# Opening of a fused attention and feed-forward kernel: one load queue in order of need, tile 1 normalised on ScalarE, tiles 2 and 3 transposed on TensorE

## The chip, the cores and the metric

The kernel runs on one core of one Trainium2 chip. The core has five engines that run their own instruction lists in order and meet through semaphores: TensorE (PE in the profile, with its weight loads listed apart as PEld), VectorE (DVE), ScalarE (ACT), GpSimd (POOL) and SyncE (SP, which here only issues transfers). The metric is the device time of one execution, in microseconds; lower is better.

## The reference

An input x of 2048 rows by 512 columns (bf16) is layer-normalised to xn. The result is x, plus a linear attention of xn, plus a gated feed-forward block of xn:

```python
xn = layernorm(x)
q, k, v = split(xn @ wqkv)                      # 32 heads of 16
phi = lambda t: where(t > 0, t + 1, exp(t)) + 1e-6
kv  = phi(k)^T v ;  z = sum over rows of phi(k) # per head
o   = (phi(q) kv) / (phi(q) z + 1e-6)
out = x + o @ wo + (silu(xn @ w_gate) * (xn @ w_up)) @ w_down   # hidden size 1792
```

The attention isn't causal: kv and z are sums over all 2048 rows, so they are known only after the last row.

## The kernel before, in words

The rows are cut into 16 tiles of 128 rows (t = 0 to 15). The work has two stages.

In the first, every tile is normalised and transposed, its K and Q projections are computed, and sums over the rows are gathered. In the second, the feed-forward block runs over 4 chunks of 512 rows (ffn, lines 545 to 575), and output tiles follow behind each chunk (outtile, line 754). The change touches only the opening of the first stage.

A small recorder, `_Prog`, takes operations in program order. K.op(engine, functions, r, w) appends them to the list of one engine and works out from the names read and written which semaphores the engine has to wait for; K.dma does the same for a transfer on the queue of an engine. No planner reorders anything: each engine runs its list in the order in which the program calls came, and a waiting instruction holds up all that stands behind it on its engine.

The steps of one tile, with their lines:

- xload (193) and wqkv_load (199) issue the transfers of x and of the K and Q weights (wk, wq, each in two halves of 256 KB). Before, they alternate between the queues of SP and ACT; the load of tiles 4 and 5 waits for tiles 0 and 1.
- stat(t) (467) is three steps: bns (274) and agg (277) on DVE give mean and variance; rstd_pow (290) gives 1/sqrt(variance + 1e-5) in two POOL instructions, vpe (an addition, line 294; for tile 0 on DVE) and rstd (a power, line 301).
- xn_dve (280) normalises the tile on DVE: (x - mean) * rstd. Tile 0 does so in two halves (xn_half, 323).
- The transposed tile xnT comes from PE and a copy out of PSUM on ACT (transpose_pe, 305, four 128x128 blocks; for tile 0 transpose_half, 333), or from a DMA transpose on SP's queue (transpose_dma, 351). Before, tiles 0 to 2 go through PE, the others by DMA; xn(t) (472) is xn_dve and, from tile 3 on, the DMA.
- kproj and qproj (391, 394) are four PE products of 512 columns each, one for each 128 rows of the weight. kb(t) and qb(t) name their PSUM banks, which alternate between 0, 1 and 2, 3.
- exp_k (397) and exp_q (403) on ACT read the banks, feat_k (431) on DVE finishes the K feature and frees the K bank, zsum (442) on POOL adds it up, gtacc (454) on PE accumulates xn^T phi(k) in banks 4 to 7.
- fill issues products on a tile of zeros (idle), whose results nobody reads.

The order of the opening is written out by hand (lines 477 to 505): statistics of tiles 0 and 1, both halves of tile 0, tile 1's normalising, statistics of 2 and 3, tile 2's normalising; then PE's list; then a loop over tiles with two tables, STAT and XN, that say behind which tile the later statistics and normalisings are issued.

Of the kernel before, what the change touches and what calls it, by code (L numbers as in the profile page):

```python
# [6 lines left out]
ACT = mybir.ActivationFunctionType  # L7
ALU = mybir.AluOpType
AX = mybir.AxisListType

P = 128
# [3 lines left out]
NT = S // P  # L15
# [93 lines left out]
def bass_parallel_sum__linear_attn_block__swiglu_ffn__prompt_kernel(  # L109
# [12 lines left out]
    K = _Prog()  # L122
    pe, act, dve, pool, sp = nc.tensor, nc.scalar, nc.vector, nc.gpsimd, nc.sync
    bf, f32 = dt.bfloat16, dt.float32

    with contextlib.ExitStack() as es:
        E = es.enter_context

        def sb(name, shape, d=bf):
            return E(nc.sbuf_tensor(name, [P] + shape, d))  # L130

        x_sb = sb("x_sb", [NT, D])
        xn_sb = sb("xn_sb", [NT, D])
# [10 lines left out]
        mv = sb("mv", [NT, 2], f32)  # L144
        vpe = sb("vpe", [NT], f32)
        rstd = sb("rstd", [NT], f32)
        nb = sb("nb", [NT], f32)
# [1 line left out]
        ek = sb("ek", [NE, D])  # L149
        eq = sb("eq", [NT, D])  # L150
        warm = sb("warm", [1], f32)
        idle = sb("idle", [512])
        pkq = sb("pkq", [NT, 2, D])
        zacc = sb("zacc", [D], f32)
        zhi = sb("zhi", [D])
# [19 lines left out]
        banks = [psum[:, i, :] for i in range(8)]  # L175
# [10 lines left out]
        def bk(i):  # L186
            return ("bank", i)
# [5 lines left out]
        def xload(eng, h, t0, n, after=()):  # L193
            K.dma(
                eng, lambda: h.dma_start(x_sb[:, t0:t0 + n, :], xv[:, t0:t0 + n, :]),
                r=list(after), w=[("x", t0 + i) for i in range(n)],
            )

        def wqkv_load(eng, h, name, i, c0, n):
            K.dma(  # L200
                eng,
                lambda: h.dma_start(
                    wqkv_sb[:, c0:c0 + n, i * D:(i + 1) * D],
                    A_wqkv[c0 * P:(c0 + n) * P, i * D:(i + 1) * D].rearrange("(c p) f -> p c f", p=P),
                ),
                w=[(name, c0)],
            )
# [4 lines left out]
        def wpiece(name, dst, src, c):  # L212
            K.dma("sp", lambda: sp.dma_start(dst[:, c, :], src[c * P:(c + 1) * P, :]), w=[(name, c)])

        xload("sp", sp, 0, 1)
        xload("act", act, 1, 1)
        wqkv_load("sp", sp, "wk", 1, 0, 2)
        wqkv_load("act", act, "wk", 1, 2, 2)
        xload("sp", sp, 2, 1)
        xload("act", act, 3, 1)  # L220
        wqkv_load("sp", sp, "wq", 0, 0, 2)
        wqkv_load("act", act, "wq", 0, 2, 2)
        xload("sp", sp, 4, 2, [("x", 0), ("x", 1)])
        xload("sp", sp, 6, 4)
        xload("sp", sp, 10, 2)
        xload("sp", sp, 12, 4)
# [8 lines left out]
                out=ident[:, :], in_=ident[:, :], compare_op=ALU.not_equal, fill=1.0,  # L235
                base=0, pattern=[[-1, P]], channel_multiplier=1,
            ),
            r=[("ident",)], w=[("ident",)],
        )
        K.op("pool", lambda: pool.memset(nhalf[:, :], -0.5), w=[("nhalf",)])  # L240
        K.op("dve", lambda: dve.memset(idle[:, :], 0.0), w=[("idle",)])

        def fill(n, after):
            K.op(
                "pe",
                [
                    (lambda: pe.matmul(banks[3], idle[:, 0:P], idle[:, :], start=True, stop=True))
                    for _ in range(n)
                ],
                r=[("idle",)] + after, w=[bk(3)],  # L250
            )

        def masks():
# [20 lines left out]
        def bns(t):  # L274
            K.op("dve", lambda: dve.bn_stats(stats[:, t, :], x_sb[:, t, :]), r=[("x", t)], w=[("st", t)])  # L275
# [4 lines left out]
        def xn_dve(t):  # L280
            K.op(
                "dve",
                lambda: dve.tensor_scalar(  # L283
                    out=xn_sb[:, t, :], in0=x_sb[:, t, :], scalar1=mv[:, t, 0:1], scalar2=rstd[:, t:t + 1],
                    op0=ALU.subtract, op1=ALU.mult,
                ),
                r=[("x", t), ("mv", t), ("rstd", t)], w=[("xn", t)],
            )

        def rstd_pow(t):  # L290
# [14 lines left out]
        def transpose_pe(t, b):  # L305
            tb = banks[b].bitcast(bf)[:, 0:512].rearrange("p (c s) -> p c s", c=NDC)
            K.op(
                "pe",
                [
                    (lambda c=c: pe.transpose(tb[:, c, :], xn_sb[:, t, c * P:(c + 1) * P], ident[:, :]))  # L310
                    for c in range(NDC)
                ],
                r=[("xn", t), ("ident",)], w=[bk(b)],
            )
            K.op(
                "act",
                lambda: act.activation(xnT[:, :, t * P:(t + 1) * P], tb, ACT.Copy),
                r=[bk(b)], w=[("xnT", t)],
            )
# [52 lines left out]
        def proj_half(t, b, lo, wname, h):  # L372
            K.op(
                "pe",
                [
                    (lambda c=c: pe.matmul(
                        banks[b], xnT[:, c, t * P:(t + 1) * P], wqkv_sb[:, c, lo:lo + D],
                        start=(c == 0), stop=(c == NDC - 1),
                    ))
                    for c in (2 * h, 2 * h + 1)  # L380
                ],
                r=[("xnTh", t, h), (wname, 2 * h)], w=[bk(b)],
            )

        def kb(t):
            return 2 * (t % 2)

        def qb(t):
            return 2 * (t % 2) + 1

        def kproj(t):
            proj(t, kb(t), D, "wk")

        def qproj(t):
            proj(t, qb(t), 0, "wq")

        def exp_k(t):
            K.op(
                "act", lambda: act.activation(ek[:, t % NE, :], banks[kb(t)], ACT.Exp),  # L399
                r=[bk(kb(t))], w=[("ek", t % NE)],  # L400
            )

        def exp_q(t):
            K.op(
                "act", lambda: act.activation(eq[:, t, :], banks[qb(t)], ACT.Exp),
                r=[bk(qb(t))], w=[("eq", t)],
            )
            K.op(
                "act", lambda: act.activation(pkq[:, t, 1, :], banks[qb(t)], ACT.Copy),
                r=[bk(qb(t))], w=[("pq", t)],  # L410
            )
# [19 lines left out]
        def feat_k(t):  # L431
            e = t % NE
            clip(ek[:, e, :], ("ek", e))
            if t >= 1:
                zsum(t - 1, e)
            maxadd(pkq[:, t, 0, :], banks[kb(t)], ek[:, e, :], [bk(kb(t)), ("ek", e)], [("pk", t)])
# [17 lines left out]
        def gtacc(t):  # L454
            K.op(
                "pe",
                [
                    (lambda c=c: pe.matmul(  # L458
                        banks[4 + c], xn_sb[:, t, c * P:(c + 1) * P], pkq[:, t, 0, :],
                        start=(t == 0), stop=(t == NT - 1),  # L460
                    ))
                    for c in range(NDC)
                ],
                r=[("xn", t), ("pk", t)], w=[bk(4 + c) for c in range(NDC)],
            )

        def stat(t):
            bns(t)
            agg(t)
            rstd_pow(t)  # L470

        def xn(t):
            xn_dve(t)
            if t >= 3:
                transpose_dma(t)

        stat(0)
        stat(1)
        xn_half(0, 0)
        xn_half(0, 1)  # L480
        xn_dve(1)
        stat(2)
        stat(3)
        xn_dve(2)

        fill(10, [])
        fill(1, [("mv", 0)])
        fill(1, [("rstd", 0)])
        transpose_half(0, 4, 0)
        transpose_half(0, 5, 1)  # L490
        fill(1, [])
        proj_half(0, kb(0), D, "wk", 0)
        proj_half(0, kb(0), D, "wk", 1)
        exp_k(0)
        transpose_pe(1, 6)
        qproj(0)
        exp_q(0)
        transpose_pe(2, 7)
        kproj(1)
        qproj(1)  # L500
        feat_k(0)
        xn(3)

        STAT = {0: (4, 5), 1: (6,), 2: (7,), 3: (8,), 4: (9, 10), 5: (11,), 6: (12,), 7: (13,), 8: (14, 15)}
        XN = {0: (4,), 1: (5,), 2: (6,), 3: (7,), 4: (8,), 5: (9, 10), 6: (11,), 7: (12,), 8: (13,), 9: (14, 15)}

        for t in range(NT):
            if t >= 2:
                kproj(t)
            if t >= 1:  # L510
                exp_k(t)
            if t >= 2:
                qproj(t)
            if t >= 1:
                exp_q(t)
                feat_k(t)
            for i in STAT.get(t, ()):
                stat(i)
            for i in XN.get(t, ()):
                xn(i)  # L520
            if t in (2, 4, 6, 8):
                wpiece("wg", wg_sb, B_w_gate, t // 2 - 1)
            if t == 11:
                for c in range(NDC):
                    wpiece("wu", wu_sb, B_w_up, c)
                wqkv_load("sp", sp, "wv", 2, 0, 4)
                wload("sp", sp, "wo", wo_sb, A_wo)
            if t == 14:
                wload("sp", sp, "wd", wd_sb, B_w_down)
            if t == 12:  # L530
                masks()
            if t >= 2:
                gtacc(t - 2)
        zsum(NT - 1, None)
        gtacc(NT - 2)
# [292 lines left out]
```

## Time and profile before

| | |
|---|---|
| median of 3 runs | 214.36 us (214.14 to 215.16) |
| profiled execution | 214.34 us, span of instructions 213.0 us |
| PE busy | 207.5 us (97%), 972 instructions |
| DVE, ACT, POOL busy | 119.4, 67.6, 72.6 us |
| moved by DMA | 16.32 MB, mean 77 GB/s |
| tile 0 of x landed | 3.3 us after its issue at 0.80 |
| first product of a projection | 7.10 us |
| granted TensorE clock | 1.00 in all 40 slices |

Times in the profile count from the first instruction. In a timeline a line gives start, length, engine, line of the kernel, operation, what is written and read, and in brackets how long the engine stood idle before and who released it. A product on PE is pipelined: its own length is 0.38 us, but the next one starts 0.216 us later, so the pitch of a group tells PE's rate. DVE and ACT overlap the start-up of neighbouring instructions in the same way.

### The profile page before, as it was taken

How to read it: one execution, taken by the hardware profiler on the slowest of the kernel's cores; microseconds unless marked ns; L12 is line 12 of the kernel's file. 1: busy time of each engine (PE TensorE's matmuls, PEld its weight loads, DVE VectorE, ACT ScalarE, POOL GpSimd, SP SyncE). 2: the span in 40 equal slices, each digit the busy share in tenths (PEclk: the TensorE clock that was granted, in tenths of full speed). 3: DMA queues.
4: the chain of work that ended last, by engine and by line, in shares of the span. 5: the costliest groups of instructions: out<-in, count | busy, mean ns of one | idle time of the engine just before them, and what ended most of it. 6: DMA issues, size and time to landing. Idle time of an engine off the chain costs nothing.

```text
span 213.0 us, 2744 instructions
## 1 busy us (share of the span) xinstructions
PE 207.5 (97%) x972; PEld 96.0 (45%) x991; DVE 119.4 (56%) x241; ACT 67.6 (32%) x117; POOL 72.6 (34%) x95
## 2 busy tenths in 40 slices
PE   7899999999999999999999999999999999999995
PEld 2344444444544444444444444444444444444454
DVE  2899997333544776446373746464556536364121
ACT  2576666667353332213122302112032213121000
POOL 1559996646013444032130442131414131221100
PEclk9999999999999999999999999999999999999999
DMA  5924598899102011110101011101011010110201
GB/s 188 388 65 125 139 143 207 287 368 266 26 0 52 0 25 25 49 24 28 31 20 49 3 35 39 49 0 49 3 49 25 25 25 28 49 25 26 51 28 51
DMA packets 26671, 16.32 MB, mean 77 GB/s; under 512 B 18592, under 2 KB 25120, under 8 KB 26656
## 3 DMA queue, kind: packets, MB, share of 16 engines
q1 hardware_dynamic: 25824, 15.34, 27.1%
q10 hardware_dynamic: 832, 0.79, 1.2%
q8 instruction: 8, 0.13, 0.3%
q14 instruction: 7, 0.06, 0.1%
HBM read 9.70 MB, written 2.10 MB: 55 GB/s over the span
## 4 chain that ended last, share of the span: by engine, by line
PE 94%; DVE 2%; DMA 2%; issue 1%; POOL 1%; DVEq 0%
PE psum L550 45%; PE psum L733 23%; PE psum L363 12%; PE psum L722 6%; PE psum L458 6%; DMA x_sb<-in_A_x_dram 2%; DVE stats L275 1%; POOL rstd L301 1%; PE psum L648 0%; PE psum L671 0%; DVE xn_sb L283 0%; DVE mv L278 0%; POOL vpe L294 0%; DVE out_sb L746 0%; PE psum L310 0%
## 5 line engine op out<-in xcount | busy, mean ns | idle before, releaser
L565 ACT ACTIVATE sg<-psum 128x512 bf16<-128x512 f32 x56 | 33.4, 598 | 106.8 <-PE psum L550 106.0
L550 PE MATMUL psum<-xnT,wu_sb 128*128 128x512 bf16 x222 | 57.4, 379 | 0.1
L550 PE MATMUL psum<-xnT,wg_sb 128*128 128x512 bf16 x217 | 56.0, 379 | 0.4
L680 POOL TENSOR_TENSOR prod<-pkq,zb 128x512 f32<-128x512 bf16 x16 | 18.6, 1161 | 57.8 <-DVE pkq L425 57.8
L550 PEld LDWEIGHTS psum<-xnT,wu_sb 128*128 128x128 bf16 x224 | 21.9, 98 | 26.4
L550 PEld LDWEIGHTS psum<-xnT,wg_sb 128*128 128x128 bf16 x224 | 21.9, 98 | 26.2
L746 DVE TENSOR_TENSOR out_sb<-psum,x_sb 128x512 bf16<-128x512 f32 (+1 forms) x17 | 11.2, 660 | 36.1 <-PE psum L733 36.1
L571 DVE TENSOR_TENSOR pkq<-psum,sg 128x512 bf16<-128x512 f32 x28 | 19.1, 686 | 18.6 <-PE psum L550 14.1
L704 POOL TENSOR_TENSOR pqn<-pkq,rden 128x512 bf16<-128x512 bf16 x16 | 16.9, 1055 | 36.6 <-DVE rden L698 36.6
L363 PE MATMUL psum<-wqkv_sb,xnT 128*128 128x512 bf16 x122 | 29.0, 379 | 0.3
L571 DVE TENSOR_TENSOR xn_sb<-psum,sg 128x512 bf16<-128x512 f32 x28 | 18.8, 671 | 14.2 <-PE psum L550 13.6
L733 PE MATMUL psum<-wd_sb,xn_sb 128*128 128x512 bf16 (+1 forms) x124 | 25.6, 355 | 0.1
L733 PE MATMUL psum<-wd_sb,pkq 128*128 128x512 bf16 x110 | 25.4, 379 | 0.1
L450 POOL TENSOR_TENSOR zacc<-zacc,pkq 128x512 f32<-128x512 f32 x15 | 17.3, 1153 | 6.9 <-DVE ek L416 6.8
L363 PEld LDWEIGHTS psum<-wqkv_sb,xnT 128*128 128x128 bf16 x124 | 12.0, 98 | 14.5 <-DMA wqkv_sb<-in_A_wqkv_dram 0.3
L733 PEld LDWEIGHTS psum<-wd_sb,xn_sb 128*128 128x128 bf16 x126 | 12.3, 98 | 11.9
L733 PEld LDWEIGHTS psum<-wd_sb,pkq 128*128 128x128 bf16 x112 | 11.0, 98 | 13.2
L722 PE MATMUL psum<-m_sb,eq 128*128 128x512 bf16 (+1 forms) x66 | 16.2, 366 | 0.1
L458 PE MATMUL psum<-pkq,xn_sb 128*128 128x512 bf16 x62 | 15.8, 379 | 0.1
L688 DVE TENSOR_REDUCE den<-prod 128x32 f32<-128x512 f32 x16 | 10.9, 683 | 5.7 <-POOL prod L680 5.7
L399 ACT ACTIVATE ek<-psum 128x512 bf16<-128x512 f32 x16 | 9.6, 598 | 9.9 <-DVE ek L416 2.8
L275 DVE BATCH_NORM_STATS2 stats<-x_sb 128x6 f32<-128x512 bf16 x16 | 10.9, 679 | 2.9 <-DMA x_sb<-in_A_x_dram 2.9
(57 smaller groups left out, 128.4 us busy)
## 6 DMA issues: line engine op xcount, KB each, us to landing
out_dram<-out_sb SPq DMA_DIRECT2D x15, 128.0 KB, 1.7
wg_sb<-in_B_w_gate_dram SPq DMA_DIRECT2D x4, 448.0 KB, 3.8
wu_sb<-in_B_w_up_dram SPq DMA_DIRECT2D x4, 448.0 KB, 4.8
wd_sb<-in_B_w_down_dram SPq DMA_DIRECT2D x1, 1792.0 KB, 13.6
x_sb<-in_A_x_dram SPq DMA_DIRECT2D x2, 512.0 KB, 6.4
wqkv_sb<-in_A_wqkv_dram ACTq DMA_DIRECT2D x2, 256.0 KB, 4.9
wqkv_sb<-in_A_wqkv_dram SPq DMA_DIRECT2D x2, 256.0 KB, 5.2
x_sb<-in_A_x_dram SPq DMA_DIRECT2D x2, 256.0 KB, 5.6
```

The costliest lines, as they stand in the source:

```text
L275: K.op("dve", lambda: dve.bn_stats(stats[:, t, :], x_sb[:, t, :]), r=[("x", t)], w=[("st", t)])
L363: (lambda c=c: pe.matmul(banks[b], xnT[:, c, t * P:(t + 1) * P], wqkv_sb[:, c, lo:lo + D], start=(c == 0), stop=(c == NDC - 1),))
L450: lambda: pool.tensor_tensor(out=zacc[:, :], in0=zacc[:, :], in1=pk, op=ALU.add),
L458: (lambda c=c: pe.matmul(banks[4 + c], xn_sb[:, t, c * P:(c + 1) * P], pkq[:, t, 0, :], start=(t == 0), stop=(t == NT - 1),))
L550: (lambda c=c: pe.matmul(banks[b], w_sb[:, c, fc * P:(fc + 1) * P], xnT[:, c, C * 512:(C + 1) * 512], start=(c == 0), stop=(c == NDC - 1),))
L565: lambda: act.activation(sg[:, j % NSG, :], banks[gb], ACT.Silu),
L571: lambda: dve.tensor_tensor(out=hT(C, fc), in0=banks[ub], in1=sg[:, j % NSG, :], op=ALU.mult,),
L680: lambda: pool.tensor_tensor(out=p, in0=pkq[:, t, 1, :], in1=zb[:, :], op=ALU.mult),
L704: lambda: pool.tensor_tensor(out=pqn[:, t % NPN, :].rearrange("p (h e) -> p h e", e=DH), in0=pkq[:, t, 1, :].rearrange("p (h e) -> p h e", ...
L722: (lambda g=g: pe.matmul(dst, pqnT(t)[:, g, :], m_sb[:, g, lo:hi], start=(g == 0), stop=False,))
L733: (lambda fc=fc: pe.matmul(dst, hT(C, fc)[:, jj * P:(jj + 1) * P], wd_sb[:, fc, lo:hi], start=False, stop=(fc == NFC - 1),))
L746: lambda: dve.tensor_tensor(out=o, in0=src, in1=x_sb[:, t, lo:hi], op=ALU.add),
```

## The change

- All loads are issued from SP, in this order: x 0, x 1, wk (first half, second half), x 2, wq (first, second half), x 3, then the rest of x. The load of tiles 4 and 5 no longer waits.
- Tile 1 is normalised by a new function, xn_act: one POOL instruction makes nb = -mean * rstd, one ACT activation (Identity) makes rstd * x + nb. It stands behind the K projection of tile 0 in the program, and so behind stat(2) and stat(3).
- Tile 2 is normalised and transposed (on PE) behind K 1; tile 3 is transposed on PE behind K 2 instead of by DMA. DMA transposes begin with tile 4.
- Statistics and normalisings of tiles 4 to 6 move ahead of the loop, which begins at tile 2.
- The products on zeros become products on a constant of ones, from a tile that the start-up code fills anyway: ten of 512 columns, five and later two of 128. They wait for nothing; before, two of them waited for tile 0's statistics.

```diff
-        idle = sb("idle", [512])
...
         xload("sp", sp, 0, 1)
-        xload("act", act, 1, 1)
+        xload("sp", sp, 1, 1)
         wqkv_load("sp", sp, "wk", 1, 0, 2)
-        wqkv_load("act", act, "wk", 1, 2, 2)
+        wqkv_load("sp", sp, "wk", 1, 2, 2)
         xload("sp", sp, 2, 1)
-        xload("act", act, 3, 1)
         wqkv_load("sp", sp, "wq", 0, 0, 2)
-        wqkv_load("act", act, "wq", 0, 2, 2)
-        xload("sp", sp, 4, 2, [("x", 0), ("x", 1)])
+        wqkv_load("sp", sp, "wq", 0, 2, 2)
+        xload("sp", sp, 3, 1)
+        xload("sp", sp, 4, 2)
...
+        def xn_act(t):
+            K.op(
+                "pool",
+                lambda: pool.tensor_scalar(
+                    out=nb[:, t:t + 1], in0=mv[:, t, 0:1], scalar1=rstd[:, t:t + 1], scalar2=-1.0,
+                    op0=ALU.mult, op1=ALU.mult,
+                ),
+                r=[("mv", t), ("rstd", t)], w=[("nb", t)],
+            )
+            K.op(
+                "act",
+                lambda: act.activation(
+                    xn_sb[:, t, :], x_sb[:, t, :], ACT.Identity, bias=nb[:, t:t + 1], scale=rstd[:, t:t + 1],
+                ),
+                r=[("x", t), ("nb", t), ("rstd", t)], w=[("xn", t)],
+            )
...
         stat(0)
         stat(1)
         xn_half(0, 0)
         xn_half(0, 1)
-        xn_dve(1)
         stat(2)
         stat(3)
-        xn_dve(2)
-        fill(10, [])
-        fill(1, [("mv", 0)])
-        fill(1, [("rstd", 0)])
+        fill(10, 512)
+        fill(5, P)
         transpose_half(0, 4, 0)
         transpose_half(0, 5, 1)
-        fill(1, [])
+        fill(2, P)
         proj_half(0, kb(0), D, "wk", 0)
         proj_half(0, kb(0), D, "wk", 1)
+        xn_act(1)
+        transpose_pe(1, 6)
         exp_k(0)
-        transpose_pe(1, 6)
         qproj(0)
         exp_q(0)
+        kproj(1)
+        xn_dve(2)
         transpose_pe(2, 7)
-        kproj(1)
         qproj(1)
+        exp_k(1)
+        exp_q(1)
+        stat(4)
         feat_k(0)
         xn(3)
+        kproj(2)
+        transpose_pe(3, 4)
+        qproj(2)
+        exp_k(2)
+        exp_q(2)
+        xn(4)
+        stat(5)
+        feat_k(1)
+        xn(5)
+        stat(6)
+        gtacc(0)
...
-        for t in range(NT):
+        for t in range(2, NT):
```

More of the change, by code (lines that the diff above doesn't have):

```diff
@@ L240, in bass_parallel_sum__linear_attn_block__swiglu_ffn__prompt_kernel, with fill @@
         K.op("pool", lambda: pool.memset(nhalf[:, :], -0.5), w=[("nhalf",)])
-        K.op("dve", lambda: dve.memset(idle[:, :], 0.0), w=[("idle",)])
-        def fill(n, after):
+        cw = nc.const_aps.tensor(1.0, (P, P), bf)
+        cx = nc.const_aps.tensor(1.0, (P, 512), bf)
+        def fill(n, cols):
             K.op(
@@ L246, in fill @@
                 [
-                    (lambda: pe.matmul(banks[3], idle[:, 0:P], idle[:, :], start=True, stop=True))
+                    (lambda: pe.matmul(banks[3][:, 0:cols], cw, cx[:, 0:cols], start=True, stop=True))
                     for _ in range(n)
                 ],
-                r=[("idle",)] + after, w=[bk(3)],
+                w=[bk(3)],
             )
@@ L473, in xn @@
             xn_dve(t)
-            if t >= 3:
+            if t >= 4:
                 transpose_dma(t)
@@ L480, in bass_parallel_sum__linear_attn_block__swiglu_ffn__prompt_kernel @@
         xn_half(0, 1)
-        xn_dve(1)
         stat(2)
         stat(3)
-        xn_dve(2)
-        fill(10, [])
-        fill(1, [("mv", 0)])
-        fill(1, [("rstd", 0)])
+        fill(10, 512)
+        fill(5, P)
         transpose_half(0, 4, 0)
         transpose_half(0, 5, 1)
-        fill(1, [])
+        fill(2, P)
         proj_half(0, kb(0), D, "wk", 0)
         proj_half(0, kb(0), D, "wk", 1)
+        xn_act(1)
+        transpose_pe(1, 6)
         exp_k(0)
-        transpose_pe(1, 6)
         qproj(0)
         exp_q(0)
+        kproj(1)
+        xn_dve(2)
         transpose_pe(2, 7)
-        kproj(1)
         qproj(1)
+        exp_k(1)
+        exp_q(1)
+        stat(4)
         feat_k(0)
         xn(3)
-        STAT = {0: (4, 5), 1: (6,), 2: (7,), 3: (8,), 4: (9, 10), 5: (11,), 6: (12,), 7: (13,), 8: (14, 15)}
-        XN = {0: (4,), 1: (5,), 2: (6,), 3: (7,), 4: (8,), 5: (9, 10), 6: (11,), 7: (12,), 8: (13,), 9: (14, 15)}
-        for t in range(NT):
-            if t >= 2:
+        kproj(2)
[9 more added lines that the diff above has]
+        gtacc(0)
+        STAT = {2: (7,), 3: (8,), 4: (9, 10), 5: (11,), 6: (12,), 7: (13,), 8: (14, 15)}
+        XN = {2: (6,), 3: (7,), 4: (8,), 5: (9, 10), 6: (11,), 7: (12,), 8: (13,), 9: (14, 15)}
+        for t in range(2, NT):
+            if t >= 3:
                 kproj(t)
-            if t >= 1:
                 exp_k(t)
-            if t >= 2:
                 qproj(t)
-            if t >= 1:
                 exp_q(t)
-                feat_k(t)
+            feat_k(t)
             for i in STAT.get(t, ()):
@@ L531, in bass_parallel_sum__linear_attn_block__swiglu_ffn__prompt_kernel @@
                 masks()
-            if t >= 2:
+            if t >= 3:
                 gtacc(t - 2)
```

## The prediction

> **What bounds the kernel now.** I read the chain of waits first, by engine and then in order of time over the first 16 us; then the busy time by stretch; then the timelines of PE, DVE and POOL over the opening; last what each DMA queue had moved. The chain by engine:
>
> ```profile
> PE 94%; DVE 2%; DMA 2%; issue 1%; POOL 1%; DVEq 0%
> ```
>
> The chain in order of time (start, length, what):
>
> ```profile
> 0.80 3.31 DMA x_sb<-in_A_x_dram
> ...
> 6.45 0.59 POOL rstd L301
> ...
> 8.76 0.58 POOL rstd L301
> ...
> 9.36 0.42 DVE xn_sb L283
> ...
> 9.83 0.40 PE psum L310 x4
> 10.23 3.45 PE psum L363 x16
> ```
>
> Up to 9.83 the end hangs on loads, statistics and normalising; from tile 2's transposes on, it hangs on PE alone. The stretches behind that point (length, then PE busy):
>
> ```profile
> 10.07:47.00 36.93, 36.72 (x171) 16.77 (x173) 28.37 (x66) 24.93 (x46) 26.73 (x42) 1.00 0.72 189
> 47.00:210.60 163.60, 162.81 (x773) 76.21 (x786) 85.37 (x159) 38.91 (x66) 42.33 (x39) 1.00 0.16 39
> ```
>
> PE is idle for 1.0 us of 200.5, so nothing behind 10.07 can be shortened by other engines. The change pays or costs what it moves the moment at which K of tile 1 starts (10.07 now), plus PE work that it puts behind that moment. PE's timeline there:
>
> ```profile
> 8.51 1.04 PE L363 MATMUL psum<-wqkv_sb,xnT 128*128 128x512 bf16 x4
> 9.83 0.40 PE L310 MATMUL psum<-ident,xn_sb 128*128 128x128 bf16 x4 [0.29 <-DVE xn_sb L283]
> 10.07 1.24 PE L363 MATMUL psum<-wqkv_sb,xnT 128*128 128x512 bf16 x5
> ```
>
> Q 0 starts at 8.51, tile 2's transposes at 9.83, K 1 0.24 later. A 512-column product takes 3.45/16 = 0.216, a projection (four) 0.86, a tile's four transposes 0.24 of PE.
>
> **The sum's base.** All durations are of the profiled execution: 214.34 us, 213.0 of them span; the median of the runs is 214.36. I add to 214.34. About 0.5% (1.07 us) is what a measurement of this kernel can tell from no change.
>
> **Where tile 1's chain goes.** The decisive edit is the one that looks smallest. Tile 1's normalising leaves DVE, where it stood ahead of the statistics of tiles 2 and 3, for a POOL instruction (nb = -mean*rstd) and a ScalarE activation. In the program both are issued after stat(2) and stat(3), and stat issues POOL work as well (vpe and rstd of its tile). POOL runs its list in order. So nb of tile 1 now stands behind rstd of tile 3, which waits for tile 3's statistics, which wait for tile 3 of x; and that load is now the eighth in the single queue, behind all of wk and wq. Behind the waiting activation on ScalarE are tile 1's copy out of PSUM and every exponential; behind tile 1's transposes on PE are Q 0, K 1 and all that follows.
>
> How long the chain is, from tile 2's own rows of DVE and POOL:
>
> ```profile
> 7.46 0.69 DVE L275 BATCH_NORM_STATS2 stats<-x_sb 128x6 f32<-128x512 bf16 x1
> 8.19 0.18 DVE L278 BATCH_NORM_AGGREGATE mv<-stats 128x2 f32<-128x6 f32 x1
> ```
>
> ```profile
> 8.46 0.22 POOL L294 TENSOR_SCALAR vpe<-mv 128x1 f32<-128x1 f32 x1 [1.43 <-DVE mv L278]
> 8.76 0.57 POOL L301 TENSOR_TENSOR rstd<-vpe,nhalf 128x1 f32<-128x1 f32 x1
> 9.30 0.22 POOL L294 TENSOR_SCALAR vpe<-mv 128x1 f32<-128x1 f32 x1
> 9.61 0.59 POOL L301 TENSOR_TENSOR rstd<-vpe,nhalf 128x1 f32<-128x1 f32 x1
> ```
>
> From the statistics' start at 7.46 to the end of rstd at 9.33 are 1.87. Let L be the moment at which tile 3 of x has landed. Statistics to rstd: L + 0.02 + 1.87. nb is an operation like vpe (0.22) with the same 0.08 of hand-over ahead: L + 2.19; the ScalarE activation starts 0.05 later, L + 2.24. For its length the nearest row is the copy of the same shape:
>
> ```profile
> L317 ACT ACTIVATE xnT<-psum 128x512 bf16<-128x512 bf16 x2 | 1.2, 598 | 0.0
> ```
>
> I take 0.60; bounds 0.41 (DVE's row for the same step) and 0.9, since no ScalarE row has a scale and a bias from memory. The Trainium skill ("ScalarE: Activation LUTs", What ACT_TABLE_LOAD costs) states that each such per-partition operand adds about 93 ns; by that estimate it would be 0.8 and the sum 0.2 longer. No row here shows it.
>
> Tile 1's transposes then start at L + 2.24 + 0.60 + 0.05 = L + 2.89. Q 0 follows after 0.24, K 1 after 0.86 more: L + 3.99. (Tile 1's copy, 0.6 behind the transposes' 0.40 with two hand-overs of 0.05, is ready at the same moment.) Tiles 2 and 3 are transposed on PE after that: 2 x 0.24 = 0.48. Before, tile 2's lay ahead of 10.07 and tile 3's was a DMA, which cost PE nothing. So the shift is
>
> L + 3.99 + 0.48 - 10.07 = L - 5.60.
>
> Break-even is L = 5.60; slower than noise from L = 6.67; faster than noise below L = 4.53.
>
> **When tile 3 lands.** What the queues had moved by 7.0 (packets, MB):
>
> ```profile
> q10 hardware_dynamic: 818, 0.78, 36.3%
> q1 hardware_dynamic: 810, 0.80, 33.5%
> ```
>
> x 0 to 3, wk and wq together are 12 x 0.131 = 1.57 MB, the bytes ahead of and including tile 3's in the new order, and both queues had moved 1.58 by 7.0. From there to landing takes the slowest of 16 engines: x 0's bytes were in at 3.6 and it landed at 4.11 (0.5 later), the last of wq landed at 8.5 (1.5 later). One queue or two share the same engines, and their busy share was 1.0 from 3.4 on, so I keep the rate. L = 7.0 + 0.5 = 7.5; latest 8.5. Earliest: bytes flow from 2.0 at the best half microsecond seen, 459 GB/s: 1.57/0.459 = 3.4, L = 5.9. SP's issuing does not bind: its four back-to-back issues show a pitch of 0.46, so the eighth goes out at 4.0.
>
> ```profile
> 4.12 1.83 SPq L195 DMA_DIRECT2D x_sb<-in_A_x_dram  x4
> ```
>
> Shift: 7.5 - 5.6 = 1.9, with bounds 0.3 and 2.9.
>
> **The clock over the hole.** K 0 still runs about as early as now (7.10) or up to 0.9 earlier, since x 0 is alone in the queue. It ends near 7.1 to 8.0, and tile 1's transposes start at 10.4: PE stands still for 2.4 to 3.3 us, with little ahead of it (idle products stop near 5.5). The widest idle stretch of the trace inside the opening is 0.4 (9.4 to 9.83), and behind it the pitch is still 0.216. The nearest row for a PE that has been standing longer is the kernel's start:
>
> ```profile
> 1.25 4.33 PE L247 MATMUL psum<-idle 128*128 128x512 bf16 x11 [1.25 <-DVE idle L241]
> ```
>
> There the pitch is 0.43 until 5.09: nine products, 9 x (0.43 - 0.216) = 1.9 us lost. A fall of the clock in the hole costs between 0 (as behind 9.83) and 1.9 (as at the start). The hole is nearer in size to the 3.8 us at the start than to 0.4, but not as long; I take half, 0.9, and keep both ends.
>
> The Trainium skill ("TensorE: Matmul & The Clock Gate", What's actually happening) says the clock falls to half after an idle window of about 3.4 us, windows running free of the kernel. By that rule the whole 1.9 falls due or none, about as likely as not: 216.2 or 218.1.
>
> **The other parts.** The idle products on a constant start at about 0.8 instead of 1.25, ahead of anything needed: 0; had they no room, they would cost 5 x 0.1. x 0 up to 1 us earlier brings K 0 forward, but the hole hides it: 0. wq, late now at 8.5 for Q 0, is needed only at 10.6: 0. The second pair of x no longer waits for the first: 0, since tile 4 is first needed behind K 3. DVE's order (stat(4) ahead of feat_k(0)) ends the first feature 1.5 behind K 1's start instead of 0.6; K 2 needs its bank 2.0 behind K 1: 0; with a slip of another 0.5 it would begin to cost. Tile 3's copy on ScalarE comes after exp_q 1, some 0.1 ahead of gtacc(0), which overwrites its bank: 0, at worst 0.5.
>
> **Sum.** 214.34 + 1.9 + 0.9 = 217.1.
>
> **Rivals.** (1) *The loads come at the trace's best rate*: L = 5.9 to 6.6, the shift is 0.3 to 1.0 and the shorter hole (0.8 to 2.4) holds the clock: 214.6 to 215.3, no change that can be told. For it: the queues ran at a share near 0.7 from 2.6 to 3.4, and SP's stood at 0.09 to 0.13 MB from 2.8 to 3.6; one queue might fill that. Against: 1 KB rows went at 300 to 390 GB/s afterwards with all engines busy. 0.14.
>
> (2) *Tile 1 free of tile 3, faster*: if nb did not wait for tile 3, tile 1 would go by its own load: with x 0 in 0.9 earlier, rstd 1 at 7.03 - 0.9 = 6.1, nb 6.45, activation to 7.05, transposes 7.1, K 1 at 8.2; 8.2 + 0.48 - 10.07 = -1.4, so 212.9. It decides where L is under 4.5; that asks for 1.57 MB in 2.0 us, 0.79 MB/us against 0.459 at best. Only the change failing to order POOL as I read it is left. 0.06.
>
> (3) *Identity needs another function table*: the load of one takes 1.28 (L230), two of them on the path 2.6: 219.7. Copy and Exp share theirs here with no load between. 0.03.
>
> **How the numbers follow.** Forecast 0.77, rivals 0.14, 0.06, 0.03. Faster 0.06, same 0.14, slower 0.80. The range takes the forecast with L from 6.6 and no loss of clock (215.3) to L = 8.5 with most of the loss (2.9 + 1.9 = 4.8, 219.1), and so a little of rival 1.
>
> **What would show it.** Right: on POOL nb of tile 1 starts after rstd of tile 3; ScalarE and PE idle until then, released by POOL; tile 3 of x lands near 7.5; K 1 starts near 11.5; pitches of 0.43 behind the hole if the clock fell. Wrong: K 1 before 10; tile 3 landed before 5.6; or new PE idle time behind K 1, which I put at none.

## The result, and the profile after

The changed kernel takes 219.53 us (219.21 to 220.40, 6 runs) against 214.37 before: a ratio of 1.024 (95% interval 1.021 to 1.027). The profiled execution is 219.31 us with a span of 217.9; 4.97 above the one of before. The prediction had the direction and the place right and the size too small: 217.1, at most 219.1.

The chain of waits after, in order of time (start, length, what):

```profile
4.20 4.79 DMA x_sb<-in_A_x_dram
8.99 0.02 issue
9.01 0.71 DVE stats L276
...
10.38 0.57 POOL rstd L319
10.95 0.10 issue
11.05 0.28 POOL nb L294
...
11.42 0.82 ACT xn_sb L302
12.24 0.05 issue
12.29 0.61 PE psum L328 x4
12.89 2.98 PE psum L381 x8
```

This is the chain that the prediction wrote down from the program alone: tile 3 of x lands, its statistics, its rstd on POOL, and only then nb of tile 1, the ScalarE activation and tile 1's transposes. POOL's timeline shows the order in which nb was held:

```profile
7.68 0.57 POOL L319 TENSOR_TENSOR rstd<-vpe,nhalf 128x1 f32<-128x1 f32 x1
10.01 0.29 POOL L312 TENSOR_SCALAR vpe<-mv 128x1 f32<-128x1 f32 x1 [1.76 <-DVE mv L279]
10.38 0.57 POOL L319 TENSOR_TENSOR rstd<-vpe,nhalf 128x1 f32<-128x1 f32 x1
11.05 0.27 POOL L294 TENSOR_SCALAR nb<-mv,rstd 128x1 f32<-128x1 f32 x1
```

Tile 1's own rstd was ready at 5.9 (it starts at 5.32 and takes 0.58); nb starts at 11.05. PE in the meantime:

```profile
6.11 1.04 PE L394 MATMUL psum<-wqkv_sb,xnT 128*128 128x512 bf16 x4 [0.25 <-ACT xnT L365]
12.29 0.61 PE L328 MATMUL psum<-ident,xn_sb 128*128 128x128 bf16 x4 [5.14 <-ACT xn_sb L302]
12.69 3.19 PE L381 MATMUL psum<-wqkv_sb,xnT 128*128 128x512 bf16 x8
15.71 0.39 PE L328 MATMUL psum<-ident,xn_sb 128*128 128x128 bf16 x4
```

K 0 came forward to 6.11, and the hole behind it is 5.14 us long. The eight products of Q 0 and K 1 then take 3.0 us from start to tile 2's transposes instead of 1.7. The stretches around them (length, busy time of PE, PEld, DVE, ACT, POOL, granted clock, DMA share, GB/s) say why:

```profile
8.40:11.80 3.40, 0.00 (x0) 0.00 (x0) 1.96 (x5) 0.38 (x1) 1.45 (x5) 1.00 0.91 356
11.80:15.30 3.50, 3.01 (x11) 1.37 (x12) 1.22 (x3) 2.18 (x5) 0.47 (x1) 0.51 0.08 31
15.30:20.00 4.70, 4.70 (x29) 2.22 (x28) 3.84 (x11) 4.29 (x9) 1.91 (x5) 1.00 0.17 35
```

The clock is at half just when work is back. Behind 20 us PE is busy all the time, so the delay is carried to the end:

```profile
47.00:215.50 168.50, 168.50 (x811) 78.55 (x810) 87.41 (x163) 42.34 (x72) 44.90 (x42) 1.00 0.19 50
```

### The profile page after: what moved, and what is told of

It reads as the page before. It is cut to its first block, busy times and chain, and to the rows that moved or that the text cites. A ratio compares the mean times of both kernels' runs of the same rounds, so it can differ in the third digit from the quotient of the medians.

```text
span 217.9 us, 2778 instructions
## 1 busy us (share of the span) xinstructions
PE 209.6 (96%) x999; PEld 96.8 (44%) x999; DVE 119.2 (55%) x239; ACT 68.7 (32%) x119; POOL 73.1 (34%) x96
## 4 chain that ended last, share of the span: by engine, by line
PE 93%; DMA 2%; SPq 1%; DVE 1%; POOL 1%; issue 0%; ACT 0%; ACTq 0%
PE psum L578 44%; PE psum L761 22%; PE psum L381 13%; PE psum L476 6%; PE psum L750 6%; DMA x_sb<-in_A_x_dram 2%; SPq L201 1%; SPq L194 1%; PE psum L328 0%; PE psum L676 0%; PE psum L699 0%; ACT xn_sb L302 0%; DVE stats L276 0%; POOL rstd L319 0%; DVE out_sb L774 0%
## 5 line engine op out<-in xcount | busy, mean ns | idle before, releaser
L578 PE MATMUL psum<-xnT,wg_sb 128*128 128x512 bf16 x224 | 57.5, 379 | 0.0
L381 PE MATMUL psum<-wqkv_sb,xnT 128*128 128x512 bf16 x124 | 30.7, 391 | 0.0
```

What stands on the lines that cost most here:

```text
L381: (lambda c=c: pe.matmul(banks[b], xnT[:, c, t * P:(t + 1) * P], wqkv_sb[:, c, lo:lo + D], start=(c == 0), stop=(c == NDC - 1),))
L578: (lambda c=c: pe.matmul(banks[b], w_sb[:, c, fc * P:(fc + 1) * P], xnT[:, c, C * 512:(C + 1) * 512], start=(c == 0), stop=(c == NDC - 1),))
```

## The experiments

The theory: nb's place on POOL ties tile 1 to tile 3's load, the load is late, and the hole lets the clock fall. Rival A: the single queue as such costs the time. Rival B: the new order, with two more tiles transposed on PE behind K 1. Rival C, for the clock alone: its fall is hidden by other engines.

**e1, nb early.** The POOL half of xn_act becomes a function of its own, issued behind stat(1); the activation stays where it was.

```diff
+        def nb_pool(t):
             K.op("pool", lambda: pool.tensor_scalar(out=nb[:, t:t + 1], ...), ...)
+
+        def xn_act(t):
             K.op("act", ...)
...
         stat(1)
+        nb_pool(1)
         xn_half(0, 0)
```

> Changed kernel, with one POOL instruction moved: nb of tile 1 is issued right behind stat(1), ahead of stat(2) and stat(3). Theory (nb stuck on POOL behind tile 3's statistics and its late load, then the clock falling in the hole): nb starts near 6.0, the ScalarE activation near 6.4, tile 1's transposes near 7.2; Q 0 then waits for the last of wq (8.6), K 1 starts near 9.5, the clock holds; 9.5 + 0.48 - 10.07 = -0.1, so about 214.2 (213.5 to 215). Rival A (the single load queue is itself the cost: late loads): 217 or more, since the loads are the same. Rival B (the new order and the transposes of tiles 2 and 3 on PE cost): 217 or more, since they are the same.

Measured: 214.80 us, ratio 1.0004 (0.998 to 1.003). One instruction in another place takes back the whole loss, with the same single queue and the same PE work, so neither rival A nor rival B makes the 5 us. nb now runs at 6.02, the activation behind it, and tile 1's transposes start at 7.25:

```profile
6.02 0.27 POOL L294 TENSOR_SCALAR nb<-mv,rstd 128x1 f32<-128x1 f32 x1
7.25 0.40 PE L330 MATMUL psum<-ident,xn_sb 128*128 128x128 bf16 x4
```

From 9 us to the end PE waits twice (us, times, longest):

```profile
PE psum L383 <- DMA wqkv_sb<-in_A_wqkv_dram: 1.3, 1, 1.3
PE psum L383 <- ACT ek L419: 0.4, 1, 0.4
```

Q 0 starts at 8.96 when wq is there and K 1 at 9.8, each some 0.3 later than written. The last 0.4 is ahead of K 2 (12.31), which writes to the bank that tile 0's feature still reads. The profile names the exponential of K 1, which ends at 12.19 and on which K 2 does not depend; the feature (DVE, 11.47 + 0.69) ends at 12.16, and in e6 the same wait is put down to it. It ends 2.3 behind K 1's start, since DVE first waits for x 3; the prediction had 1.5, with a limit of 2.0.

**e2, two queues.** The loads as before, the rest as changed.

```diff
-        xload("sp", sp, 1, 1)
+        xload("act", act, 1, 1)
...                                        # second halves of wk and wq likewise
-        xload("sp", sp, 3, 1)
+        xload("act", act, 3, 1)           # sixth to go out
```

> Changed kernel, loads alone put back as before (two queues, x 3 sixth to go out on ScalarE's queue). Theory: x 2 lands near 7.05 and x 3 at 6.8 as before, so tile 3's statistics start near 7.9 instead of 9.01; tile 1's transposes near 11.2 instead of 12.3, still behind rstd of tile 3; 1.1 less than the changed kernel if the clock falls alike, 2.5 less if the clock holds over a hole of 3.2: 217 to 218.4. Rival A (the single queue is itself the cost): back to 214.4 to 215. Rival B (order and PE transposes): 219 as the changed kernel.

Measured: 217.69 us, ratio 1.013 (1.010 to 1.016). The loads are not the cost, but their moment counts: tile 1's transposes start at 10.44, 1.85 ahead of the changed kernel, and the time is 1.84 less (1.68 between the two profiled executions). They start earlier than I wrote, since tile 2 of x landed sooner than before. The clock fell here too, behind a hole of only 2.39:

```profile
10.44 0.40 PE L328 MATMUL psum<-ident,xn_sb 128*128 128x128 bf16 x4 [2.39 <-ACT xn_sb L302]
10.67 3.05 PE L381 MATMUL psum<-wqkv_sb,xnT 128*128 128x512 bf16 x8
```

**e3, the hole filled.** Idle products ahead of tile 1's transposes; the chain is untouched.

```diff
+        fill(22, 512)
         xn_act(1)
         transpose_pe(1, 6)
```

> Changed kernel, with 22 idle products of 512 columns on PE between K 0 and tile 1's transposes (4.75 us at full pitch, in a hole of 5.1), so that PE isn't idle there. Tile 1's chain is the same. Theory: transposes still at 12.3, but the products behind them at a pitch of 0.216 from the start: 1.4 to 1.5 less than the changed kernel, 217.9 in all. Rival C (the clock's fall is hidden by ScalarE and DVE being late anyway): no difference, 219.3. If the fills delay the transposes: 219.3 or more.

Measured: 218.17 us, ratio 1.015 (1.012 to 1.018), 1.36 under the changed kernel, with the clock at 1.00 throughout. In this execution x 3 landed at 9.41 and the transposes start at 12.70, later than in the changed kernel, and the kernel is faster nonetheless:

```profile
12.70 0.40 PE L328 MATMUL psum<-ident,xn_sb 128*128 128x128 bf16 x4 [0.33 <-ACT xn_sb L302]
13.15 1.67 PE L381 MATMUL psum<-wqkv_sb,xnT 128*128 128x512 bf16 x7
14.66 0.39 PE L328 MATMUL psum<-ident,xn_sb 128*128 128x128 bf16 x4
```

From tile 1's transposes to tile 2's it takes 1.96 instead of 3.42: the fallen clock costs 1.46 in that execution of the changed kernel. Rival C falls.

**e4, x 3 ahead of wq**, still in one queue.

```diff
         xload("sp", sp, 2, 1)
+        xload("sp", sp, 3, 1)
         wqkv_load("sp", sp, "wq", 0, 0, 2)
         wqkv_load("sp", sp, "wq", 0, 2, 2)
-        xload("sp", sp, 3, 1)
```

> Changed kernel, one load moved: x 3 goes out directly behind x 2, ahead of both halves of wq. The queue is still single. Theory: x 2 lands at 6.3 as now, x 3 near 6.9; tile 3's statistics start near 7.2 instead of 9.0; tile 1's transposes near 10.5; the time falls by the same 1.8, and by up to 1.5 more if the clock holds over a hole of 3.5: 216.0 to 217.6. Rival A (single queue as such): 219, unchanged. Rival B (order and PE transposes): 219, unchanged.

Measured: 218.71 us, ratio 1.017 (1.013 to 1.020), above what I wrote. The chain did nearly as expected (transposes at 10.69), yet only 0.8 of its 1.6 arrived. In the profiled execution the granted clock was at half for twice as long:

```profile
9.10:15.90 6.80, 5.21 (x19) 2.45 (x20) 3.28 (x8) 3.71 (x7) 2.10 (x6) 0.50 0.53 198
```

It fell 1.7 us behind the end of K 0 (7.44), while PE still stood idle. Two of the four executions have a mean clock that fits one stretch of 3.4 (0.992); they took 217.8 and 218.6.

**e8, the same with the hole filled.** Since this reading of e4 came after the fact, it was put to a test.

```diff
+        fill(14, 512)
         xn_act(1)
```

> e4 (x 3 ahead of wq) with 14 idle products of 512 columns (3.0 us) between K 0 and tile 1's transposes. Theory: e4 came out 1.1 above its upper expectation's middle because the clock was at half from 9.1 to 15.9, two windows, not because of the chain, whose transposes start at 10.7 as in e4; with PE kept busy the clock holds: 10.7 + 1.1 + 0.48 - 10.07 = 2.2, less some 0.3 given back later: 216.0 to 216.8. Rival (something else is late in e4, wq or a bank): 217.5 or more.

Measured: 216.19 us, ratio 1.008 (1.005 to 1.010), 2.5 under e4, with the same start of the transposes (10.61) and the clock at 1.00. So e4's excess was the clock, and with the clock held the time follows the landing of x 3: from e3 to e8 the transposes move from 12.70 to 10.61 (2.1), the time by 2.0.

**e5, the single queue alone** in the kernel before (the load lines of the change, nothing else).

> Kernel before, with the changed kernel's load order alone: all loads from SP's queue, x 3 eighth; everything else as before. Theory (tile 1 hung behind tile 3, plus the clock): tile 1 is free here, but DVE takes tile 3's statistics ahead of tile 2's normalising, so tile 2's transposes wait for x 3, which lands near 9.0 to 9.4: normalising at 9.9 to 10.3 instead of 9.36, K 1 at 10.5 to 10.9 instead of 10.07; 214.8 to 215.2, with the clock held. Rival A (the single queue as such makes the 5 us): 217.5 or more.

Measured: 215.44 us, ratio 1.003 (1.001 to 1.005): 0.2 above the range that I wrote, though its cost of 0.7 against before lies within the 0.5 to 0.9 that this range added to 214.34. Tile 3's statistics, which stand ahead of tile 2's normalising on DVE, wait for x 3:

```profile
9.24 0.69 DVE L275 BATCH_NORM_STATS2 stats<-x_sb 128x6 f32<-128x512 bf16 x1 [1.67 <-DMA x_sb<-in_A_x_dram]
```

K 1 starts at 10.74, 0.67 later than before. That this alone makes the 0.7 is not shown: in the profiled execution (215.66) PE also stands 0.85 ahead of K 9, at 31.64, a wait that the profile of before does not have.

**e6, tile 1 on DVE** again, the rest as changed: xn_dve(1) behind tile 0's halves, no xn_act.

> Changed kernel, with tile 1 normalised on DVE where it was before (behind tile 0's halves, ahead of stat(2)); no nb, no ScalarE activation. Theory: tile 1 needs only its own rstd (5.9): normalised by 6.4, transposed right behind K 0 near 7.1; Q 0 waits for wq (8.7 to 8.9), K 1 near 9.6; the clock holds; like e1, 214.2 to 215. Rival B (new order and PE transposes): 217 or more. If ScalarE as such were the cost of e1's tie, this would be 0.4 or more under e1.

Measured: 214.85 us, ratio 0.9998 (0.998 to 1.001), as e1. Normalising on ScalarE was not itself the cost: in both, PE waits for wq at that point (1.55 here) and tile 1 is ready before. PE also waits 0.50 ahead of K 2 for tile 0's feature.

**e7 and e9, looking for a version that beats both.** e7 is e6 with K 1 and tile 2's transposes ahead of Q 0, and tile 2's normalising and tile 0's features ahead of stat(3). e9 also moves tile 5's normalising and the statistics of tile 6 behind tile 2's features, and the statistics and normalisings of tiles 7 and 8 one step later.

> A version meant to beat both: tile 1 on DVE as in e6, K 1 and tile 2's transposes ahead of Q 0 on PE (wk lands 3 us ahead of wq), tile 2 normalised ahead of stat(3), features of tile 0 ahead of stat(3). Theory: K 1 at 8.1, tile 2's transposes at 8.9, Q 0 at 9.2 when wq is there, then PE without a gap; Q 2 ends near 12.9 instead of 13.5: 213.7 (213.2 to 214.3). Rival: a new wait takes it back (tile 3's normalising behind x 3 at 9.4, near 12.0, holds its transposes): 214.4 or more.

> e7 with one wait taken out: the profile of e7 shows K 4 held 0.64 by the feature of tile 2, which stood on DVE behind tile 5's normalising and tile 6's statistics. Here tile 5's normalising and the statistics of 6 go behind tile 2's features, those of 7 and 8 one step later. Theory: gtacc(0) starts at 13.4 as in e7, 0.1 ahead of before, and PE runs without a gap behind it: equal to before or up to 0.5 faster, 213.9 to 214.6. Rival: DVE is short of time there, and another tile's normalising or DMA transpose becomes late: 215 or more.

Measured: e7 215.20 us, ratio 1.003 (1.001 to 1.005); e9 214.94, ratio 1.002 (0.999 to 1.004). Neither is faster, and both are above the times hoped for. K 1 starts at 8.41 and 8.22, near the 8.1 written, but in e7 PE waits 0.64 for a feature at K 4:

```profile
17.66 1.89 PE L381 MATMUL psum<-wqkv_sb,xnT 128*128 128x512 bf16 x8 [0.64 <-DVE pkq L443]
```

The execution of e7 that was profiled is the slowest of its ten (216.57), and 1.43 of it is another wait, ahead of K 9. In e9 the wait at K 4 is gone and gtacc(0) starts at 13.84; PE then waits 0.5 ahead of the transposes for tiles 2 and 3 to be normalised, and 1.0 ahead of K 6 and K 9.

The profile puts the waits ahead of K 9 down to ScalarE's copy of a Q projection (e5, e9) or to nothing (e7). K 9 does not depend on that copy, which had ended half a microsecond earlier. It needs tile 9's DMA transpose: issued at 25.4, 26.1 and 25.9 in e5, e7 and e9, it landed 6.1, 6.0 and 5.6 later, some 0.1 ahead of K 9 each time (31.64, 32.21 and 31.59). In e1, where PE doesn't wait there, it took 4.7. Likewise K 6 in e9 starts (22.89) when tile 6's transpose has landed (issued at 19.9, 3.0 to landing). That a DMA transpose becomes late was the rival written for e9; why it took longer there stays open. No version here beats the kernel before.

## Why the prediction was right or wrong

**Right: the mechanism.** nb behind rstd of tile 3, ScalarE and PE idle until then, a hole behind K 0, a pitch of 0.43 after it. All were named from the program's order and rows of the profile before, and e1 shows the first to be the cause. No new PE idle time behind K 1 was forecast, and there is none.

**Wrong: the size of three terms of the sum**, all in the same direction.

1. *The landing of x 3: 7.5 forecast (8.5 at the latest), 8.99 measured; 1.5.* This is the largest miss, and it has two parts. I kept the rate of two queues. Bytes moved by 7.0 (packets, MB, share of the engines) after, then in e5, where one queue is the only change, then in e2, where the two queues are back:

```profile
q1 hardware_dynamic: 1447, 1.38, 65.3%
```

```profile
q1 hardware_dynamic: 1380, 1.31, 63.0%
```

```profile
q1 hardware_dynamic: 846, 0.82, 38.0%
q10 hardware_dynamic: 791, 0.75, 33.5%
```

The 1.57 MB that were in at 7.0 with two queues were in at about 7.6 with one. And from the bytes to the landing I took 0.5, the lag of the first load; it was 1.4, near the 1.5 of the last of wq, which I had put down as the worst case. A load deep in a queue should have been sized by the row of a load deep in a queue.

2. *From the landing to tile 1's transposes: 2.89 forecast, 12.29 - 8.99 = 3.30 measured; 0.4.* Half is the activation: 0.82 on the path against the 0.60 that I took from a copy without operands from memory. The rest is POOL (vpe 0.30 where the row had 0.22, nb 0.28) and the hand-overs. The estimate by the Trainium skill ("ScalarE: Activation LUTs", What ACT_TABLE_LOAD costs), which the prediction set beside the 0.60, came to 0.8; e1, e2 and e3 show 0.81 too.

3. *The clock: 0.9 forecast as half of a range, 1.46 measured* (e3). The hole was 5.14, since K 0 came forward and x 3 came late, not 2.4 to 3.3. Its 1.46 lay within the 1.9 that bounded it. The Trainium skill ("TensorE: Matmul & The Clock Gate", What's actually happening) has the clock fall after an idle window of about 3.4 us, counted from a window that runs free. The half-clock stretches, 3.4 us here and 6.8 in e4, agree with that length. But in e2 it fell behind an idle stretch of 2.39, and in e4 after 1.7 us of idling: an idle stretch as long as the window isn't needed.

Corrected by the three, the sum is 1.9 + 0.9 + 1.5 + 0.4 + 0.6 = 5.3. DVE's last step, right behind PE's last product, indeed starts 5.2 later (215.87 against 210.64). The span grows by 4.9, since from there to the end it took 2.0 instead of 2.4; that 0.3 wasn't forecast, and no run here explains it.

**The range.** Its top, 219.1, already added the latest landing to the whole loss of the clock (2.9 + 1.9 = 4.8; the prediction calls it most of the loss). 219.5 lay 0.4 beyond, and not because of the clock, which cost less than its 1.9: x 3 landed 0.5 later than the bound called latest, and the range had nothing for the 0.4 of the chain, though the prediction had put bounds of 0.41 and 0.9 on the activation.

**The rivals.** The loads at the trace's best rate, and tile 1 free of tile 3, did not occur. ScalarE's function table was not reloaded ahead of Identity. The parts costed at nothing were nothing on the path of the changed kernel, where PE waits for nothing more behind the hole. With the hole gone two of them come up: in e1 PE waits 1.30 for wq and 0.4 for tile 0's feature. The tie of e1 with before hides one gain and one loss: x 0 lands at 2.2 behind its issue instead of 3.3, and K 0 starts at 6.25 instead of 7.10; wq in the one queue then holds Q 0 until 8.96, later than the 8.51 of before. This is also what rival 2 had left out: it started K 1 at 8.2 and came to 212.9, but ahead of K 1 stands Q 0, which needs wq. e1 brings about its condition and gains nothing.

## What to carry to other kernels

When a step moves to another engine, list every instruction that it issues and what stands ahead of each in that engine's list; the place of a helper of 0.27 us on POOL cost more than the work that it helps. Put loads in the order in which the in-order engines reach their consumers, which need not be the order in which the main engine uses them. Where a change opens a hole on TensorE, price the hole and the clock together: waits of 1.3 and 1.6 us left the clock whole here (e1, e6), holes of 2.4, 3.3 and 5.1 halved it for a while (e2, e4, the changed kernel).

## What the runs showed of the hardware that I had not expected

One queue moved 1.23 to 1.38 MB by 7.0 us in the eight profiles with a single queue that I read there (the changed kernel, e1 and e3 to e8), two queues 1.57 and 1.58 (e2, before), though the first load of the single queue landed sooner (2.2 to 2.6 us after its issue, against 3.2 and 3.3). In the changed kernel most of the difference arises from 5 to 7 us: 248 and 282 GB/s in these two microseconds, against 317 and 366 before. Why the single queue is slower there stays open.

The granted clock fell behind an idle stretch of PE of 2.39 us (e2) and after 1.7 us of idling (e4), and stayed at half for 3.4 or 6.8 us, most of it while PE was already busy again. Executions of the changed kernel with a mean clock of 0.992 took 219.2 to 219.3 us, those with 0.984 219.4 to 220.4. The profiled execution is of the first kind, so the 1.46 above is what one stretch at half clock cost.
